# Batch 2's keys and values loaded as two halves, the second added by an accumulating DMA; query halves interleaved with expert weights; weight forms moved to other slots of the vector engine

## The chip, the cores and the metric

The kernel runs on one core of one Trainium2 chip. The metric is the device time of one execution in microseconds (us). Five engines share the work: PE (the tensor engine, matmuls), DVE (vector), ACT (scalar), POOL (GpSimd) and SP (which here only issues transfers). Sixteen DMA engines move the data.

A ratio is the mean time of one kernel's fast runs over the mean of the other's fast runs of the same rounds on the same chip. So it is not quite the ratio of the medians that stand beside it.

## The reference, cut to what matters

```python
# B=8 batches, H=8 heads, S=576 tokens, D=64
k_p = k.reshape(B, H, 72, 8, D).mean(axis=3)      # keys: mean over 8 rows
v_p = v.reshape(B, H, 72, 8, D).mean(axis=3)
attn = softmax(q @ k_p^T / sqrt(D))               # 576 x 72 per head
x = (attn @ v_p)  as (B*S, H*D) = (4608, 512)
# then 4 experts over all 4608 tokens
for e in range(4):
    h = relu(x @ w1[e])                           # 512 -> 1024
    out += p[:, e:e+1] * (h @ w2[e])              # 1024 -> 512
```

## The kernel before

Tokens go through in batches of 512 and each batch through four experts. While the experts of one batch run on PE, the attention of the next is prepared on the other engines. Products with 2x2 blocks are done with seven block products instead of eight, so sums of the blocks of w1, w2, x and h ("forms") are computed beside the matmuls, on DVE and POOL. A form is due only at the step that uses it, but DVE also empties the PSUM banks (the memory into which the matmuls write) that PE needs next, so a form in a bad slot can stall PE.

Batches and experts are numbered from 0, as in the code. The keys and values of a batch are 72 partitions of 8 heads x 8 rows x 64 numbers. The mean over 8 rows is a chain of additions, 8 rows to 4, to 2, to 1. Before the change, batch 2 loads all 8 rows at once and has one addition more; later batches already load rows 0 to 3 and let a second DMA add rows 4 to 7 on landing:

```python
def load_kv(b, src, nm):           # whole: values into the w2_t space of experts 2 and 3
    wide = (w2_t[0:SP, 2:4]... if nm == "vraw" else raw_kv...)
    nc.gpsimd.dma_start(out=raws[(nm, b)], in_=src[b]...)

def load_half(b, src, nm, half):   # halves: both into raw_kv, the second accumulating
    raws[(nm, b)] = raw_kv[:, 0 if nm == "kraw" else 1]
    lo = half * POOL // 2
    nc.gpsimd.dma_start(
        out=raws[(nm, b)],
        in_=src[b].rearrange("h (j r) d -> j h r d", r=POOL)[:, :, lo:lo + POOL // 2],
        accum_op=ALU.add if half else ALU.bypass,
    )

def combine_w2(e, engine=nc.vector):   # four forms of w2(e), 128x1024 each
    return [lambda: sub(out=t1, in0=b12, in1=b11),
            lambda: sub(out=t2, in0=b22, in1=t1),
            lambda: sub(out=t4, in0=b21, in1=t2),
            lambda: sub(out=b12, in0=b22, in1=b12)]     # t1, t2, t4 live in w2_t[:, e]
```

The start-up queues all first loads on GpSimd, in this order at its end:

```python
load_w1(3)
load_w2(2)
load_q_halves(1)
load_v(1)
...
```

Batch 1's attention sits at numbered points of expert 3 of batch 0. The last steps make batch 1's tokens (`context`), and SP transposes them with four DMA transposes into xT, which PE needs for the next step:

```python
43: [lambda: fold_keys(1, hi), lambda: load_k(2)],
...
60: [lambda: scores(1, 3)],                               # s == 3 adds here, on GpSimd:
    # pool_waits(vps[1]), load_v(2), combine_w2(1, nc.gpsimd)
61: [lambda: context(1, 0), lambda: turn(1, 0)],          # turn: DMA transpose x_tok -> xT
64: ...  67: ...
69: [lambda: context(1, 3), lambda: turn(1, 3)],

def up_plain(c, e, fcs):     # first expert of batch 1: 32 matmuls that read all of xT
    ...
    nc.tensor.matmul(h_ps[:], lhsT=w1_bf[...], rhs=xT[:, kc, :], ...)
```

The softmax here doesn't subtract the row's maximum and nothing guards it: scores larger than these inputs give would overflow.

## Time and profile before

| | before |
|---|---|
| median of 3 runs | 503.62 us (502.55 to 504.42) |
| span of the profiled run | 501.7 us |
| PE busy | 490.9 us, 98% |
| granted PE clock | 1.00 |

In the timeline a row has the start, the duration, the engine, the line of code, the operation, output and inputs, and in brackets the idle time just before and what ended it. "SPq" and "POOL ... DMA" rows are issues of transfers, not the transfers themselves. This is the timeline of the kernel before:

```profile
66.92 0.85 POOL L88 DMA_DIRECT2D w_t<-in_v_dram  x1
...
69.91 5.21 SPq L425 DMA_TRANSPOSE xT<-x_tok  x3
...
75.79 1.23 SPq L425 DMA_TRANSPOSE xT<-x_tok  x1
...
78.65 7.07 PE L686 MATMUL h_ps<-xT,w_bf 128*128 128x512 bf16 x31
```

GpSimd issues one load, the whole of batch 2's values, at 66.92. SP then issues the four transposes of batch 1's tokens. By the DMA completions in the trace (the moment at which a transfer has fully arrived, "landed" from here on) the load landed at 76.55 and the last transpose at 78.52. PE reaches the next expert just then, at 78.65, with no wait on record: the transposes end on the critical path, the chain of work that sets the end time, with no slack.

### The profile page before, as it was taken

How to read it: one execution, taken by the hardware profiler on the slowest of the kernel's cores; microseconds unless marked ns; L12 is line 12 of the kernel's file. 1: busy time of each engine (PE TensorE's matmuls, PEld its weight loads, DVE VectorE, ACT ScalarE, POOL GpSimd, SP SyncE). 2: the span in 40 equal slices, each digit the busy share in tenths (PEclk: the TensorE clock that was granted, in tenths of full speed). 3: DMA queues.
4: the chain of work that ended last, by engine and by line, in shares of the span. 5: the costliest groups of instructions: out<-in, count | busy, mean ns of one | idle time of the engine just before them, and what ended most of it. 6: DMA issues, size and time to landing. Idle time of an engine off the chain costs nothing.

```text
span 501.7 us, 11093 instructions
## 1 busy us (share of the span) xinstructions
PE 490.9 (98%) x4537; PEld 397.5 (79%) x4547; DVE 362.1 (72%) x651; ACT 290.0 (58%) x541; POOL 196.0 (39%) x177
## 2 busy tenths in 40 slices
PE   8999999999999999999999999999999999999996
PEld 3746554797788888888788888887888888888884
DVE  1367886899987767777777777777777767776674
ACT  3654444765666567665766576666655565556650
POOL 8473360458323562267126722661115111512110
PEclk9999999999999999999999999999999999999999
DMA  9999999684925373836573287433210110012003
GB/s 118 206 205 205 202 182 169 77 105 49 140 57 93 47 76 105 109 48 61 110 119 49 23 136 89 65 40 63 65 22 1 54 43 12 1 43 64 2 1 84
DMA packets 84770, 41.90 MB, mean 84 GB/s; under 512 B 48736, under 2 KB 80224, under 8 KB 84720
## 3 DMA queue, kind: packets, MB, share of 16 engines
q0 software_dynamic: 43216, 22.91, 36.2%
q1 hardware_dynamic: 41104, 17.77, 17.1%
q8 instruction: 35, 0.57, 0.5%
q10 hardware_dynamic: 400, 0.52, 0.3%
q14 instruction: 15, 0.12, 0.1%
HBM read 45.69 MB, written 9.44 MB: 110 GB/s over the span
## 4 chain that ended last, share of the span: by engine, by line
PE 82%; DMA 9%; DVE 4%; POOL 2%; issue 1%; ACT 1%; POOLq 0%; ACTq 0%
PE u_ps L790 37%; PE g_ps L668 37%; DMA w_bf<-in_moe_w_dram 5%; DMA q_sb<-in_q_dram 3%; PE o_ps L884 3%; PE two L280 2%; PE two L403 1%; PE h_ps L686 1%; DMA H_sb<-in_v_dram 1%; DVE acc L774 1%; POOL w_bf L154 1%; DVE H_sb L716 1%; DVE w_t L658 0%; DVE w_t L656 0%; PE o_ps L899 0%
## 5 line engine op out<-in xcount | busy, mean ns | idle before, releaser
L668 PEld LDWEIGHTS <-w_bf 128*128 128x128 bf16 x1848 | 178.7, 98 | 26.4 <-issue 1.3
L774 DVE SCALAR_TENSOR_TENSOR acc<-u_ps,p_all,acc 128x512 f32<-128x512 f32 (+1 forms) x216 | 127.6, 592 | 70.2 <-ACT u_ps L827 65.9
L736 POOL TENSOR_TENSOR h_s<-H_sb,h_s 128x1024 bf16<-128x1024 bf16 x31 | 66.0, 2128 | 240.9 <-DVE h_s L735 228.4
L668 PE MATMUL g_ps<-xT,w_bf 128*128 128x256 bf16 x928 | 129.9, 273 | 0.0
L668 PE MATMUL g_ps<-xf,w_bf 128*128 128x256 bf16 x792 | 109.3, 272 | 0.6 <-DVE H_sb L716 0.2
L790 PEld LDWEIGHTS <-H_sb 128*128 128x128 bf16 x992 | 92.5, 98 | 20.1 <-issue 6.0
L712 ACT COPY r<-g_ps 128x512 f32<-128x512 f32 x136 | 79.7, 586 | 41.4 <-PE g_ps L668 34.3
L790 PE MATMUL u_ps<-w_bf,H_sb 128*128 128x256 bf16 x744 | 102.0, 273 | 0.0
L716 DVE CUSTOM_DVE_ANT_0 H_sb<-g_ps,r 128x512 bf16<-128x512 f32 x136 | 93.5, 687 | 2.8 <-ACT r L712 2.5
L719 ACT ACTIVATE H_sb<-g_ps 128x512 bf16<-128x512 f32 x128 | 76.3, 597 | 18.5 <-PE g_ps L668 18.2
L790 PEld LDWEIGHTS <-h_s 128*128 128x128 bf16 x744 | 72.8, 98 | 8.4
L811 ACT COPY g_ps<-g_ps 128x512 f32<-128x512 f32 x62 | 35.4, 570 | 73.5 <-PE g_ps L668 73.5
L790 PE MATMUL u_ps<-w_t,h_s 128*128 128x256 bf16 x496 | 74.4, 273 | 0.0
L827 ACT COPY u_ps<-u_ps 128x256 f32<-128x256 f32 x62 | 22.2, 358 | 34.1 <-PE u_ps L790 33.7
L790 PE MATMUL u_ps<-w_t,H_sb 128*128 128x256 bf16 x248 | 37.3, 273 | 1.3 <-DVE acc L774 1.3
L790 PE MATMUL u_ps<-w_bf,h_s 128*128 128x256 bf16 x248 | 37.2, 273 | 0.0
L884 PE MATMUL o_ps<-w_bf,H_sb 128*128 128x512 bf16 x145 | 35.6, 379 | 0.5 <-issue 0.2
L284 ACT ACTIVATE expT<-two 72x1024 bf16<-72x1024 f32 x28 | 28.5, 1016 | 0.0
L829 DVE TENSOR_SCALAR acc<-u_ps,p_all 128x512 f32<-128x512 f32 x16 | 12.0, 750 | 19.5 <-ACT u_ps L827 19.5
L884 PEld LDWEIGHTS <-H_sb 128*128 128x128 bf16 x152 | 14.3, 98 | 14.1 <-issue 0.8
L733 DVE TENSOR_TENSOR h_s<-H_sb 128x1024 bf16<-128x1024 bf16 x31 | 21.1, 681 | 2.7 <-ACT H_sb L690 2.7
L394 DVE TENSOR_TENSOR x_tok<-two,inv 128x512 bf16<-128x512 f32 x32 | 22.1, 691 | 1.1
(125 smaller groups left out, 446.9 us busy)
## 6 DMA issues: line engine op xcount, KB each, us to landing
out_dram<-acc SPq DMA_DIRECT2D x32, 256.0 KB, 2.4
w_bf<-in_moe_w_dram POOLq DMA_DIRECT2D x17, 256.0 KB, 8.9
w_bf<-in_moe_w_dram POOLq DMA_DIRECT2D x8, 512.0 KB, 14.5
q_sb<-in_q_dram POOLq DMA_DIRECT2D x6, 512.0 KB, 9.8
raw_kv<-in_k_dram POOLq DMA_DIRECT2D x10, 288.0 KB, 6.7
raw_kv<-in_v_dram POOLq DMA_DIRECT2D x10, 288.0 KB, 6.3
raw_kv<-in_k_dram POOLq DMA_DIRECT2D x2, 576.0 KB, 15.1
w_t<-in_v_dram POOLq DMA_DIRECT2D x2, 576.0 KB, 12.4
```

The lines of the kernel that those rows point to most:

```text
L284: nc.scalar.activation(out=state[("expT", b)][:, 2 * pair:2 * pair + 2].rearrange("j h r s p -> j s (h r) p"), in_=two[0:SP].rearrange("j ...
L394: nc.vector.tensor_tensor(out=x_tok, in0=c_ps[:, :, :, 0:D], in1=inv[:].unsqueeze(3).to_broadcast([P, 2, NPAIR, D]), op=ALU.mult,)
L668: nc.tensor.matmul(bank[:, t, :], lhsT=w1_bf[:, e, block, kc, lo:lo + P], rhs=x[:, kc, :], start=(first and t == 0 and kc == 0), stop=(t = ...
L712: nc.scalar.copy(out=r[:], in_=ps[:])
L716: nc.vector._custom_dve(TENSOR_ADD_SAT, out=out, in0=ps[:], in1=r[:], s0=BIG, s1=0.0)
L719: nc.scalar.activation(out=out, in_=ps[:], func=ACT.Relu)
L736: lambda: nc.gpsimd.tensor_sub(out=s4, in0=a12, in1=s2),
L774: nc.vector.scalar_tensor_tensor(out=acc, in0=ps, scalar=prob, in1=acc, op0=ALU.mult, op1=ALU.add,)
L790: nc.tensor.matmul(out, lhsT=lhs[0][:, lhs[1] + f, lhs[2]], rhs=rhs[0][:, rhs[1] + f, rhs[2]], start=(start and f == 0), stop=(f == FCH // ...
L811: nc.scalar.copy(out=s[:], in_=g[:])
L827: nc.scalar.copy(out=two[:, hi], in_=one[:, lo])
L884: nc.tensor.matmul(sums[r][:], lhsT=hidden[(c, e)][:, fc, r * P:(r + 1) * P], rhs=w2_bf[:, e, fc, :], start=(fc == 0), stop=(fc == FCH - 1),)
```

## The change

There are three intents. The queries of batch 1 should arrive earlier, by interleaving their halves with the halves of w2(2). Batch 2's keys and values should come as halves, as in later batches, which saves four DVE additions and frees the w2_t space of experts 2 and 3 early. With that space free, the forms of w2(2) and w2(3) can leave the two DVE slots at 116.8 and 130.7 us, where they collide with GpSimd and stall PE. The diff, cut to its core (the split of two load functions into halves is left out):

```diff
-            43: [lambda: fold_keys(1, hi), lambda: load_k(2)],
+            43: [lambda: fold_keys(1, hi), lambda: load_half(2, k, "kraw", 0)],
 ...
-            add(6, *key_parts(b)[:2])
-            add(7, *key_parts(b)[2:])
-            add(7, lambda: keys(b))
+            add(6, *key_parts(b)[:1])
+            add(7, *key_parts(b)[1:])
+            add(7, lambda: keys(b), *combine_w2(2))
 ...
-                add(9 + n, part)
+                add(10 + n, part)
 ...
-        load_w2(2)
-        load_q_halves(1)
+        for half in range(2):
+            load_w2_half(2, half)
+            load_q_half(1, half)
 ...
-                    [lambda: pool_waits(vps[1][0:1, H - 1, 0:1]), lambda: load_v(2)]
-                    + combine_w2(1, nc.gpsimd))
+                    [lambda: pool_waits(vps[1][0:1, H - 1, 0:1]), lambda: load_half(2, k, "kraw", 1),
+                     lambda: load_half(2, v, "vraw", 0)] + combine_w2(1, nc.gpsimd)
+                    + [lambda: load_half(2, v, "vraw", 1)])
 ...                                                     # s == 5, 6, 7
-                w2f = combine_w2(2)
-                forms_due.extend(nothing[:3] + u[3:] + w2f[:1] + nothing[:2] + w2f[1:2])
+                v3 = combine_w2(3)
+                forms_due.extend(nothing[:3] + u[3:] + v3[:1])
-                v3 = combine_w2(3)
-                forms_due.extend(nothing[:3] + w2f[2:] + nothing[:2] + v3[:1])
+                forms_due.extend(nothing[:3] + v3[3:] + v3[1:2])
-                forms_due.extend(nothing[:3] + v3[3:] + v3[1:2] + nothing[:2] + v3[2:3])
+                forms_due.extend(nothing[:3] + v3[2:3])
```

Also gone is the first addition (8 rows to 4) in `fold_parts`.

More of the change, by code (lines that the diff above doesn't have):

```diff
@@ L125, in load_first_q, with load_q_half @@
         )
-    def load_q_halves(b):
-        raws[("q", b)] = qpool.tile([P, H, NR, D], BF16, name="q_sb")
-        for hs in halves:
-            nc.gpsimd.dma_start(
-                out=raws[("q", b)][:, hs].rearrange("p h r d -> p h (r d)"),
-                in_=q[b, hs, 0:NT, :].rearrange("h (p r) d -> p h (r d)", r=NR),
-            )
+    def load_q_half(b, half):
+        if half == 0:
+            raws[("q", b)] = qpool.tile([P, H, NR, D], BF16, name="q_sb")
+        hs = halves[half]
+        nc.gpsimd.dma_start(
+            out=raws[("q", b)][:, hs].rearrange("p h r d -> p h (r d)"),
+            in_=q[b, hs, 0:NT, :].rearrange("h (p r) d -> p h (r d)", r=NR),
+        )
     def load_q_rem(b):
@@ L157, in load_w1, with load_w2_half @@
                 )
+    def load_w2_half(e, half):
+        rows = moe_w2[e].rearrange("(fc p) d -> p fc d", p=P)
+        fcs = slice(half * FCH // 2, (half + 1) * FCH // 2)
+        nc.gpsimd.dma_start(out=w2_bf[:, e, fcs], in_=rows[:, fcs])
     def load_w2(e):
-        rows = moe_w2[e].rearrange("(fc p) d -> p fc d", p=P)
-        for lo in (0, FCH // 2):
-            fcs = slice(lo, lo + FCH // 2)
-            nc.gpsimd.dma_start(out=w2_bf[:, e, fcs], in_=rows[:, fcs])
+        for half in range(2):
+            load_w2_half(e, half)
     def reload_w2(e):
@@ L218, in fold_parts @@
     def fold_parts(nm, b, hs, last, engine):
-        def first():
-            raw = raws[(nm, b)]
-            engine.tensor_add(out=raw[:, hs, 0:4, :], in0=raw[:, hs, 0:4, :],
-                                 in1=raw[:, hs, 4:8, :])
         def rest():
@@ L230, in rest @@
                 engine.tensor_add(out=out, in0=raw[:, hs, 0, :], in1=raw[:, hs, 1, :])
-        return [first, rest] if b == 2 else [rest]
+        return [rest]
     def key_parts(b):
@@ L967 @@
         load_w1(3)
-        load_w2(2)
-        load_q_halves(1)
+        for half in range(2):
+            load_w2_half(2, half)
+            load_q_half(1, half)
         load_v(1)
```

## The prediction

> **What bounds the kernel now.** I read the page first, then the waits of the tensor engine, then the timeline of the stretches that the diff touches.
>
> ```profile
> PE 490.9 (98%) x4537; PEld 397.5 (79%) x4547; DVE 362.1 (72%) x651; ACT 290.0 (58%) x541; POOL 196.0 (39%) x177
> ```
>
> The tensor engine (PE) is busy for 490.9 of 501.7 us at a granted clock of 1.00. The diff changes no matmul, so only time in which PE stands still can be won. The waits of PE alone, longest first:
>
> ```profile
> PE u_ps L790 <- DVE acc L774: 1.3, 2, 0.8
> PE o_ps L501 <- DVE x_rem L939: 1.3, 1, 1.3
> PE one L380 <- DMA H_sb<-in_v_dram: 0.9, 1, 0.9
> PE qt_ps L338 <- DMA q_sb<-in_q_dram: 0.7, 1, 0.7
> ...
> PE g_ps L668 <- DVE H_sb L716: 0.2, 1, 0.2
> ```
>
> The second and third belong to the first 14 us, which the diff leaves alone. The first, fourth and last lie where it works. A pipelined matmul is recorded as 273 ns but followed by the next after 109 ns (8 in 0.87 us in the chain), so a stall is about 0.16 us longer than its idle time. Counted from start to start, PE loses 0.88 us at 56.1 (first half of batch 1's queries not landed), 0.38 at 93.5, 0.98 + 0.16 at 118.7 and 0.57 + 0.16 at 133.1 (0.66 there, less the 0.09 that every score matmul costs). Together **3.1 us, 0.6% of the time**: the ceiling of this change.
>
> The timeline around the longest of them, VectorE (DVE), GpSimd (POOL) and PE together (start, duration, engine, line):
>
> ```profile
> 116.34 2.11 POOL L736 TENSOR_TENSOR h_s<-H_sb,h_s 128x1024 bf16<-128x1024 bf16 x1 [1.23 <-DVE h_s L735]
> ...
> 116.77 2.23 DVE L656 TENSOR_TENSOR w_t<-w_bf 128x1024 bf16<-128x1024 bf16 x1
> ...
> 118.92 0.74 DVE L774 SCALAR_TENSOR_TENSOR acc<-u_ps,p_all,acc 128x512 f32<-128x512 f32 x1
> ...
> 119.72 0.60 PE L790 MATMUL u_ps<-w_t,H_sb 128*128 128x256 bf16 x4 [0.82 <-DVE acc L774]
> ```
>
> A form of w2(3) on DVE starts 0.43 us after GpSimd's own subtraction and takes 2.23 us instead of 0.68. It ends 0.55 us after GpSimd does. The accumulation behind it frees the PSUM bank that PE wants, so PE stands. At 130.74 the same happens to the next form (2.23 us, PE at 133.69).
>
> **What the Trainium skill says.** "SBUF — State Buffer", section "Who interferes with whom": a VectorE instruction with two SBUF inputs contends with a GpSimd instruction that reads SBUF, and the one that comes later is blocked for the whole of the other. The trace agrees: 2.23 against 0.68 us. "DMA: Bandwidth & Descriptors", "Queues, rings and completion order": descriptors start in ring order on each of 16 engines, which take turns between queues packet by packet. The trace agrees: the 16 completions of a load spread over some 5.5 us and the last ones come in order of issue, and a transpose of x_tok issued at 69.91 beside queued loads landed after 6.48 us, one issued at 75.79 after 2.73. Same page, "Rules for kernel authors": an accumulating transfer must wait for the semaphore of an earlier one to the same bytes. The trace agrees: GpSimd idled 6.15 us before the second half of batch 3's keys at 99.66, until the first half had landed. No page gives the accumulation's price; here such loads landed 6.5 to 9.4 us after issue against 5.0 to 7.3 for first halves.
>
> **The change part by part** (numbers of batches and experts as in the code, from 0; the halves concern index 2).
>
> *Queries interleaved with w2(2).* By the completions in the trace the two halves of w2(2) landed at 53.06 and 55.61, the query halves at 56.96 and 58.28. The queue moves about 200 KB per us without a pause until 75 us. So a half of w2 costs 2.55 us, a query half 1.35. In the new order: w2 half 53.06, query half 54.4, w2 half 56.96, query half 58.28. The first transposes no longer wait (PE gets there at 56.13), but the second want their half at about 57.5 and **it lands at 58.28 as before**, since the same bytes are ahead of it. They started at 58.41 before. I give this part 0.1 us, and 0.15 more for an earlier DVE copy that removes most of a 0.32 us gap at 60.6. Total 0.25 of the 0.88.
>
> *Halves instead of folds.* Four DVE additions of 72x1024 go, 0.68 us each, 2.7 us. DVE is no bound. On PE's path is only what delays it at 93.45: the value folds (0.68 at 91.44) push L716, which ends at 93.89 and holds PE's bank. Without one fold it ends near 93.2 and PE's 0.38 us go. Values now live in raw_kv, so the w2_t space of experts 2 and 3 is free some 30 us earlier, and that allows the next part.
>
> *Forms in other slots.* All four of w2(2) go into the DVE gap before L733; one of w2(3) into the slot at 95, two into those at 108 (0.68 us each there now), the last to 122. The slots at 116.8 and 130.7 become empty: **PE wins 1.14 + 0.73 = 1.87 us**. At 122 two forms, 0.81 and 1.64 us beside GpSimd's work, already run without a PE stall, so one will too.
>
> *The price, between 70 and 88 us.* The gap that receives w2(2) is this one:
>
> ```profile
> 86.39 0.69 DVE L733 TENSOR_TENSOR h_s<-H_sb 128x1024 bf16<-128x1024 bf16 x1 [2.71 <-ACT H_sb L690]
> 87.11 0.69 DVE L734 TENSOR_TENSOR H_sb<-H_sb 128x1024 bf16<-128x1024 bf16 x1
> ```
>
> Four forms at 0.69 are 2.75 us; two folds less give back 1.36; net 1.39 of 2.71, which fits by itself. But GpSimd shifts. The second half of the keys must wait for the first, which I put at 71.67 (landing of the whole now) less half of 2.92, so 70.2. GpSimd is in order: 70.3, plus 1.4 and 0.85 for two issues, plus 4 x 2.13 for the forms of w2(1), ends at 81.1 instead of 76.4. DVE's work from 78.6 on has two SBUF inputs and collides: L637 and the first fold may lose up to one GpSimd instruction each. I estimate 1 to 3 us lost, so DVE reaches L733 0 to 1.7 us late. PE needs L734's result at 87.86 and waits for all that is late. The second halves also move while batch 1's xT transposes are in flight; PE starts the next expert at 78.65, 0.13 us after the last of them landed, so a later landing costs directly: estimate 0 to 0.8. Together 0 to 2.5, middle **1.1 us lost**.
>
> Sum: 0.25 + 0.38 + 1.87 - 1.1 = 1.4 us won. From 503.6 that is 502.2.
>
> **The rivals.** (a) All stalls go and nothing new appears: 3.1 us, 500.5. For it: the net DVE work falls. Against it: the byte count ahead of the second query half. (b) The stall moves instead of going: new waits at 78 and 88 us eat all of the gain, or more: 503.6 to 504.5. For it: GpSimd's later end and the tight xT landing. Against it: DVE's gap of 2.71 us. (c) The accumulating loads arrive so late (after 80 us) that the key fold, the transpose of the keys and the scores at 87.5 slip together: over 505. The 9.4 us of one such load beside transposes speaks for it; that nothing but these loads is left in the queue after 75 speaks against. (d) DMA becomes lighter and everything early wins: no, the bytes are the same.
>
> **Range and chances.** Certain gains of 2.25 us (93, 118, 133) less 0 to 2.5, plus 0.25, gives 501.1 to 503.6; the runs of before spread by 0.9 us either way, so I widen to 500.7 to 503.9. A change of 2% is 10 us, more than three times the ceiling; slower by that would need a new wait of 10 us, which nothing shows. Faster 0.005, same 0.985, slower 0.01.
>
> **What would show it.** In the new profile: the wait of L338 for the queries stays at about 0.6 us but before the second transposes; L656 and L658 of w2 on DVE all near 0.7 except one; no PE idle time near 118 and 133; L716 at 93 no longer holds PE; the idle time of DVE before L733 is gone or small, and PE idles before L790 near 88 if I am right about GpSimd ending near 81. I am wrong if PE shows no new wait between 77 and 89 (then it is faster, near 501), or if L280 or L686 wait there for DMA (then slower).

## More of the kernel before

The windows view gives busy time by engine for a stretch, and at the end of a row the granted clock, the DMA share and the GB/s moved (192 GB/s is 192 KB per us; all DMA queues together). Of the kernel before:

```profile
68.00:72.00 4.00, 3.89 (x35) 2.37 (x35) 3.52 (x8) 1.04 (x2) 3.92 (x2) 1.00 1.43 192
72.00:75.00 3.00, 2.87 (x26) 1.32 (x26) 2.40 (x6) 0.00 (x0) 2.92 (x3) 1.00 1.37 167
```

The queue is full here: 192 and 167 KB per us.

## The result, and the profile after

| | before | after |
|---|---|---|
| median of 4 runs each | 503.75 us | 506.69 us |
| lowest to highest | 502.55 to 504.42 | 506.01 to 507.36 |
| span of the profiled run | 501.7 us | 504.4 us |

The ratio is 1.0061 (95% interval 1.0034 to 1.0088). By the 2% rule this is "same", but the change made the kernel slower by 3 us, and the time lies above the predicted range (500.7 to 503.9).

The page of the kernel after, busy time of each engine and the granted PE clock in 40 slices:

```profile
PE 491.5 (97%) x4537; PEld 397.7 (79%) x4547; DVE 356.6 (71%) x647; ACT 289.9 (57%) x541; POOL 198.0 (39%) x179
...
PEclk9999998999999999999999999999999999999999
```

DVE has 5.5 us less to do, as intended. PE has the same matmuls. One slice of the clock, the seventh, shows an 8: something happened between 76 and 88 us. The waits of PE from 50 to 160 us (total, times, longest), of the kernel after, say what:

```profile
PE h_ps L685 <- DMA xT<-x_tok: 3.9, 1, 3.9
PE qt_ps L337 <- DMA q_sb<-in_q_dram: 0.3, 1, 0.3
```

The waits behind the vector engine that the prediction showed (1.3 and 0.2 us) are gone. One new wait of 3.9 us stands in their place: the first matmul of batch 1's first expert waits for xT. The timeline of the kernel after, in the same stretch as above:

```profile
66.24 0.18 POOL L251 COPY mark<-vp 1x1 bf16<-1x1 bf16 x1 [5.75 <-DVE vp L256]
...
69.42 1.42 POOL L95 DMA_DIRECT2D raw_kv<-in_k_dram  x1 [2.99 <-DMA raw_kv<-in_k_dram]
69.47 5.94 SPq L424 DMA_TRANSPOSE xT<-x_tok  x3
...
70.30 1.39 POOL L95 DMA_DIRECT2D raw_kv<-in_v_dram  x1
...
76.09 1.25 SPq L424 DMA_TRANSPOSE xT<-x_tok  x1
...
82.22 8.35 PE L685 MATMUL h_ps<-xT,w_bf 128*128 128x512 bf16 x31 [3.95 <-DMA xT<-x_tok]
```

GpSimd is ready at 66.42, but the accumulating half of the keys must not start before the first half has landed (68.79 by the completions). It stands for 2.99 us. Meanwhile nothing is queued behind it, and the windows view of the kernel after shows the queue running dry:

```profile
68.00:72.00 4.00, 3.93 (x35) 2.27 (x34) 3.52 (x7) 0.60 (x2) 2.58 (x3) 1.00 0.78 99
72.00:75.00 3.00, 2.88 (x26) 1.52 (x28) 2.40 (x7) 0.00 (x0) 2.92 (x2) 1.00 0.95 78
...
80.00:82.00 2.00, 0.00 (x0) 0.00 (x0) 0.00 (x0) 0.00 (x0) 1.51 (x2) 0.85 0.97 313
```

From 68 to 75 us the DMA engines moved 4 x 99 + 3 x 78 = 630 KB, against 4 x 192 + 3 x 167 = 1269 KB before. The two loads issued at 69.42 and 70.30 landed at 76.21 and 80.50; the four transposes, issued at nearly the same times as before, landed at 73.60, 80.69, 81.05 and 82.08, where before they had landed at 76.39, 77.04, 77.45 and 78.52.

The clock of 0.85 in the last of these rows is the second loss. One tile's view, of xT in the kernel after (shortest, median and longest duration in ns, first and last start):

```profile
L685 PE MATMUL h_ps<-xT,w_bf x31: 379/379/631, 82.2 to 90.2; 128*128 128x512 bf16 x31
```

The first seven matmuls after the wait run at about half rate, so that the group takes 8.35 us in place of 7.07. Of the four runs, two (507.33 and 507.36 us) had a granted clock of 0.992 against 0.997 in the other two, the profiled one among them; so they ran longer at half rate than this trace shows.

The balance of PE in the two profiled runs, counted from start to start between one matmul and the next, before against after:

| place (us, before) | before | after | difference |
|---|---|---|---|
| 56 to 58, queries | 0.95 | 0.46 | -0.49 |
| 60, copy of the queries | | | -0.04 |
| 78, xT | 0.11 | 4.11 | +4.00 |
| 79, half rate | 0 | 1.28 | +1.28 |
| 93, value folds | 0.38 | 0 | -0.38 |
| 118, form beside GpSimd | 1.14 | 0 | -1.14 |
| 133, form beside GpSimd | 0.73 | 0 | -0.73 |
| sum | | | +2.5 |

The spans differ by 2.7 us; some 0.1 us of the rest lies in the first 14 us.

At 118 the intended gain is seen as planned, in the timeline of the kernel after:

```profile
120.79 2.12 POOL L735 TENSOR_TENSOR h_s<-H_sb,h_s 128x1024 bf16<-128x1024 bf16 x1 [1.23 <-DVE h_s L734]
...
122.04 0.75 DVE L773 SCALAR_TENSOR_TENSOR acc<-u_ps,p_all,acc 128x512 f32<-128x512 f32 x1 [0.74 <-ACT u_ps L826]
...
125.54 1.51 DVE L657 TENSOR_TENSOR w_t<-w_bf,w_t 128x1024 bf16<-128x1024 bf16 x1
```

DVE has nothing to do while GpSimd subtracts, so it is there in time for the accumulation (it waits 0.74 us for ACT). Only one form, at 125.54, still runs beside GpSimd and takes 1.51 us, and PE does not notice.

### The profile page after: what moved, and what is told of

Read it like the earlier page. It is cut to its first block, busy times and chain, and to the rows that moved or that the text cites. A ratio compares the mean times of both kernels' runs of the same rounds, so it can differ in the third digit from the quotient of the medians.

```text
span 504.4 us, 11092 instructions
## 1 busy us (share of the span) xinstructions
PE 491.5 (97%) x4537; PEld 397.7 (79%) x4547; DVE 356.6 (71%) x647; ACT 289.9 (57%) x541; POOL 198.0 (39%) x179
## 4 chain that ended last, share of the span: by engine, by line
PE 85%; DMA 9%; POOL 3%; issue 1%; ACT 1%; DVE 1%; POOLq 0%; ACTq 0%
PE u_ps L789 38%; PE g_ps L667 38%; DMA raw_kv<-in_k_dram 3%; DMA w_bf<-in_moe_w_dram 3%; PE o_ps L883 3%; DMA q_sb<-in_q_dram 3%; PE two L279 2%; PE h_ps L685 2%; PE two L402 1%; DMA xT<-x_tok 1%; POOL w_bf L155 1%; POOL H_sb L107 1%; POOL w_bf L163 0%; POOL q_sb L122 0%; PE o_ps L898 0%
## 5 line engine op out<-in xcount | busy, mean ns | idle before, releaser
L732 DVE TENSOR_TENSOR h_s<-H_sb 128x1024 bf16<-128x1024 bf16 x31 | 21.1, 681 | 2.8 <-ACT H_sb L689 2.8
```

## The experiments

**My theory after the result.** The accumulating load makes GpSimd wait for the first half; the queue runs dry; its loads then overlap the four transposes, xT lands late, and the wait lets the clock fall. **Rivals:** the query interleave (or some other reordering) delays everything behind it; the accumulation itself is slow, whenever it is issued; the transposes are late for a reason that has nothing to do with the loads. Two questions of size go with it: what the half rate costs, and what the forms' new slots are worth alone.

The first four kernels ran on one chip, beside seven runs of the kernel before (median 503.41).

### e1_q_only: the query interleave alone

```diff
 (kernel before)
-        load_w2(2)
-        load_q_halves(1)
+        for half in range(2):
+            load_w2_half(2, half)
+            load_q_half(1, half)
```

> The kernel before with nothing but the interleaving of batch 1's query halves with w2(2). If the queries' part is as the changed kernel's trace has it, the wait before the first query transposes (0.88 us from start to start) goes, one of 0.4 to 0.5 us appears before the second, and nothing new appears near 78 us: 503.2 to 503.6. If the interleaving itself delays the transposes of x_tok (the rival), the tensor engine waits over 1 us before the expert that starts near 78 us and the time is over 505.

The median was 504.02 us (503.2 to 503.6 expected), the ratio 1.001 (0.9995 to 1.0026): no change that the noise lets through. The first query transposes no longer waited. The second ones started at 58.49, against 58.41 before, still held by the landing of their half. The bytes ahead of that half are the same, so nothing is won at its end. The stalls at 118 and 133 are there as before, and there is no wait for xT. So the interleave is cleared of the loss.

### e2_plain_k: the change, with a plain second half of the keys

The second half of batch 2's keys overwrites the first instead of being added. The keys are wrong (the output stays within the tolerance of the comparison). The wait for the first half stays, since both write the same bytes.

```diff
 (kernel after, load_half)
-            accum_op=ALU.add if half else ALU.bypass,
+            accum_op=ALU.add if half and (b, nm) != (2, "kraw") else ALU.bypass,
```

> The changed kernel with one word different: the second half of batch 2's keys is written over the first instead of added to it (wrong result on purpose; same bytes, same issue, same waits). Theory A (the accumulation is what is slow: it moved about 90 KB per us where plain loads moved 190, and holds the transposes of x_tok behind it): the loads end near 76 us, the last transpose lands by 79.5, the wait of 3.95 us falls under 1.5 and the time to 502 to 503.5. Theory B (any bytes that are issued at 69 to 71 us collide with the transposes, added or not): the wait stays above 3 us and the time at 505.5 to 507.

The median was 503.98 us, the ratio 1.0012 (0.9986 to 1.0037). The waits of PE:

```profile
PE h_ps L685 <- DMA xT<-x_tok: 2.8, 1, 2.8
PE two L279 <- DMA kpT<-kp: 0.6, 1, 0.6
```

2.8 of the 3.95 us are left with a plain load issued late. The loads landed at 78.81 and the last transpose at 80.19, which is 1.9 us earlier than in the kernel after, but PE was there 0.7 us earlier too (77.55 against 78.27). The result lies between the marks of both theories (under 1.5, over 3 us). In this pair of traces the accumulation has a share of 1 to 2 us, and the rest of the wait remains without it; how far one trace can be trusted is said below the table of runs. The matmuls behind this wait ran at full rate (7.07 us). A second wait appears, for the transpose of the keys before the first scores.

### e3_no_v_half: the first half of the values not loaded

The half at 70.30 is left out, and the remaining half of the values is loaded after the forms of w2(1). The result is wrong (relative error 0.23).

```diff
 (kernel after, point 60)
-                    [..., lambda: load_half(2, k, "kraw", 1),
-                     lambda: load_half(2, v, "vraw", 0)] + combine_w2(1, nc.gpsimd)
-                    + [lambda: load_half(2, v, "vraw", 1)])
+                    [..., lambda: load_half(2, k, "kraw", 1)] + combine_w2(1, nc.gpsimd)
+                    + [lambda: load_half(2, v, "vraw", 0)])
```

> The changed kernel without the first value load at 70.3 us: batch 2's values are moved as one half only, after GpSimd's forms of w2(1) (wrong result on purpose). The accumulating key load stays. Theory A (accumulation): the key load alone still holds the transposes, the wait before the expert near 78 us stays above 2 us, 504.5 to 506. Theory B (bytes at that time): half of the bytes are gone, the wait falls under 1.5 us, 501.5 to 503.5.

The median was 502.63 us, the ratio 0.9986 (0.9969 to 1.0004).

```profile
PE h_ps L685 <- DMA xT<-x_tok: 0.5, 1, 0.5
```

With one load fewer in front, the last load lands at 76.09, xT at 78.33, and 0.5 us of the wait is left. So the bytes that go in late, not the transposes themselves, hold xT up. How much of the wait they make is less sure: e7 below is the same program up to this point, and there PE waited 2.0 us.

### e4_fill: the wait filled with matmuls on zeros

Eighteen matmuls that add nothing stand where PE waits, so that PE is busy although xT is as late as before.

```diff
 (kernel after, s == E, j == 1)
+                        warm(18)
                         up_plain(c, e, range(FCH))
```

> The changed kernel with 18 matmuls on zeros in the tensor engine's wait before the expert near 78 us (18 x 0.216 = 3.9 us). Theory: the 7 matmuls at half rate after the wait (about 0.21 us lost each, 1.2 to 1.4 us in all) come from the engine's idle time; with the idle time filled they run at full rate, the wait for the transposes stays the same and the time falls by 1.0 to 1.4 us, to 505.3 to 505.7. Rival: the slow matmuls come from something else at that time (the transposes' traffic): the time stays or grows.

The median was 506.02 us, the ratio 1.0052 (1.0035 to 1.007). The timeline:

```profile
78.78 4.05 PE L500 MATMUL o_ps<-x_rem 128*128 128x512 bf16 x18
...
82.67 7.07 PE L685 MATMUL h_ps<-xT,w_bf 128*128 128x512 bf16 x31
```

The group behind the wait takes 7.07 us again: all 1.28 us of the half rate are gone at that place. In the times this saving is not shown: the median is 0.7 us below that of the kernel after (1.0 to 1.4 expected), and the intervals of the two ratios overlap. In e4's profiled run the wait for the queries was 1.05 us against 0.29, which hides a part.

The next four kernels ran on a second chip, beside eleven runs of the kernel before (median 503.93).

### e5_whole_forms: values whole as before, forms in the new slots

Keys and values are loaded as in the kernel before. The values are put at another offset, so that three forms of w2(2) can run in the gap near 86 us. The rest of the forms go so that the slots at 116.8 and 130.7 stay empty.

```diff
 (kernel before, with the query interleave)
+        at = FCH * TH if b == 2 else 0
-        wide = (w2_t[...][:, 0:H * POOL * D] if nm == "vraw"
+        wide = (w2_t[...][:, at:at + H * POOL * D] if nm == "vraw"
 ...
-            add(7, lambda: keys(b))
+            w2f = combine_w2(2)
+            add(7, lambda: keys(b), w2f[0], w2f[1], w2f[3])
 ...                                                     # s == 5, 6, 7
+                forms_due.extend(nothing[:3] + u[3:] + nothing[:3] + combine_w2(2)[2:3])
+                forms_due.extend(nothing[:3] + v3[:2])
+                forms_due.extend(nothing[:3] + v3[3:] + v3[2:3])
```

> The forms of w2(2) and w2(3) moved without the loads in halves: batch 2's keys and values come whole, as before (the values at the other end of the same space, so that three of the four forms of w2(2) fit into DVE's idle time before L733); queries interleaved as in the first experiment. Theory: the moved forms are worth what the prediction gave them, and only the halved loads cost. No waits near 118 and 133 us (1.14 + 0.73 us less than before), the 0.38 at 93 stays, no wait over 0.6 us at the expert near 78 us: 501.0 to 502.2 against 503.4. Rival (DVE gets late in its filled gap and the tensor engine waits near 88 us instead): a wait of 1 us or more at L734's result, and 503 or over.

The median was 502.48 us, the ratio 0.9975 (0.9962 to 0.9988). The waits of PE from 50 to 160 us:

```profile
PE g_ps L676 <- DVE H_sb L724: 0.5, 2, 0.3
PE u_ps L798 <- DVE acc L782: 0.2, 1, 0.2
```

No wait for xT. The stalls at 118 and 133 are gone, and waits of 0.2, 0.3 and 0.2 us for DVE remain near 94, 115 and 127. So the forms' new slots are worth having by themselves, and they need no halves.

### e6_k_early: the change, with the first half of the keys ahead of three other loads

```diff
 (kernel after)
-        load_w2(3)
-        load_q_rem(0)
-        load_q_rem(1)
 ...
-            43: [lambda: fold_keys(1, hi), lambda: load_half(2, k, "kraw", 0)],
+            43: [lambda: fold_keys(1, hi), lambda: load_half(2, k, "kraw", 0),
+                 lambda: load_w2(3), lambda: load_q_rem(0), lambda: load_q_rem(1)],
```

> The changed kernel with the first half of batch 2's keys queued ahead of w2(3) and the remaining queries, instead of behind them. Bytes, accumulation and the rest are the same; the second half need not wait for the first any more and is issued near 66.5 us instead of 69.4, into a queue that is still full. Theory (the queue ran empty while GpSimd waited for the first half, and the two loads came 3 us late, beside the transposes): the last load lands by 77.5, the wait of 3.95 us falls under 1.5, no matmuls at half rate, the time 501.5 to 503.5. Rival (the accumulating load holds the transposes wherever it is issued): the wait stays over 2.5 us and the time over 504.5.

The median was 503.81 us (502.5 to 506.05, six runs; 501.5 to 503.5 expected), the ratio 1.0007 (0.999 to 1.0025), clear of the kernel after's 1.0034 to 1.0088. GpSimd no longer waits: the second half is issued at 67.00 and the values' half at 67.89. The waits of PE:

```profile
PE h_ps L686 <- DMA xT<-x_tok: 1.2, 1, 1.2
PE two L279 <- DMA kpT<-kp: 0.3, 1, 0.3
```

Issuing early takes 2.75 of the 3.95 us away, and xT lands 2.6 us earlier (79.52). 1.2 us stay although the issue is as early as the whole load of before. In the windows view the stretch from 72 to 75 moved 126 KB per us, between the 78 of after and the 167 of before.

### e7_v_late: both halves of the values behind the forms of w2(1)

```diff
 (kernel after, point 60)
-                     lambda: load_half(2, v, "vraw", 0)] + combine_w2(1, nc.gpsimd)
-                    + [lambda: load_half(2, v, "vraw", 1)])
+                    ] + combine_w2(1, nc.gpsimd)
+                    + [lambda: load_half(2, v, "vraw", 0), lambda: load_half(2, v, "vraw", 1)])
 ...
-                add(10 + n, part)
+                add(14 + n, part)
```

> The changed kernel with both halves of batch 2's values issued after GpSimd's forms of w2(1), and their folds four slots later. Theory (the value half is what the transposes wait for, as in the third experiment): the wait falls to 0.5 to 1 us; with the other gains, 501.5 to 503.5. If the late second half (near 93 us) is not there for its fold near 99, a new wait on DVE shows there.

The median was 508.7 us, the ratio 1.0097 (1.0075 to 1.012): a miss. The waits of PE from 70 to 110 us:

```profile
PE two L402 <- DVE vp L229: 3.1, 1, 3.1
PE h_ps L685 <- DMA xT<-x_tok: 2.0, 1, 2.0
```

I had expected 0.5 to 1 us for xT; it was 2.0, since the accumulating half of the keys alone, issued at 70.42, still took until 78.17. (e3, the same program up to here, issued it at 69.03; it landed at 76.09, and PE waited 0.54.) The larger wait, 3.1 us, is of my own making, as the timeline of e7 shows:

```profile
104.36 2.16 POOL L735 TENSOR_TENSOR h_s<-H_sb,h_s 128x1024 bf16<-128x1024 bf16 x1 [1.46 <-DVE h_s L734]
104.58 2.09 DVE L229 TENSOR_TENSOR vp<-raw_kv 72x256 bf16<-72x256 bf16 x1
```

The values' second half had landed at 95.77. But I had moved the folds back by four points to make room for it, and there the last one meets GpSimd's subtraction and takes 2.09 us instead of 0.29. This is the collision of 118 us once more, with PE behind it. It cost more than its length: from 105.86 to 112.69 us the granted clock was 0.50, in which matmuls followed each other after 213 ns instead of 109, an estimate of 3 us more. So e7's time says nothing against late values as such; its wait for xT says that one accumulating half issued at 70 can be enough for 2 us.

### e8_fold_early: e5 with the value folds spread over other points

```diff
 (e5_whole_forms)
-            for n, part in enumerate(value_parts(b)):
-                add(9 + n, part)
+            for n, part in zip((8, 9, 11, 12), value_parts(b)):
+                add(n, part)
```

> The fifth experiment with the first fold of the values one slot earlier, in DVE's idle microsecond before L829, and the two folds of the other half one slot apart from it. Theory: the 0.38 us that the tensor engine loses at 93 us goes too, 0.3 to 0.4 less than the fifth: 500.7 to 501.9. Rival: the fold collides with GpSimd's subtraction that starts at 88.9, and DVE is late for L829: no gain, or 0.3 us worse.

The median was 501.88 us (500.91 to 502.62), the ratio 0.9962 (0.9948 to 0.9976). This beats both kernels; against e5 the intervals overlap. In the trace the stall at 93 is gone too. This profiled run did show one wait for xT, whose last transpose landed at 78.57:

```profile
PE h_ps L694 <- DMA xT<-x_tok: 0.8, 1, 0.8
```

Its loads are those of e5, which showed no wait, and its xT landed at the same time as there (78.57, 78.67). But PE had lost less in the first 60 us (in e5's profiled run the granted clock was 0.50 from 15.8 to 19.2 us) and began its last group before xT at 73.65, against 74.92 in e5. So up to this point the queue sets the pace by the clock on the wall, and PE that comes earlier only waits. This also bounds what any gain ahead of 78 us can be worth, the queries' included.

The last two ran on a third chip, beside seven runs of the kernel before (median 503.38).

### e9_extra_load: the kernel before with one useless plain load

If late bytes in front of the transposes are the cause, then a plain load of 288 KB that nobody reads must do the same to the kernel before. It has no accumulation and no wait for an earlier half. It is issued at 69.49, beside the transposes.

```diff
 (kernel before)
+    def load_extra():                      # half of v[2] into unused bytes of w2_t
+        nc.gpsimd.dma_start(out=spare..., in_=v[2]...[:, :, 0:POOL // 2])
 ...
-                    + combine_w2(1, nc.gpsimd))
+                    + combine_w2(1, nc.gpsimd)[:1] + [load_extra] + combine_w2(1, nc.gpsimd)[1:])
```

> The kernel before with one load added that nothing uses: half of batch 2's values (288 KB, plain) into free space, issued near 70 us between GpSimd's first and second form of w2(1). No accumulation, no wait for an earlier half, no other change. Theory (bytes of the GpSimd queue beside the transposes are the cause): the last load lands 1.5 to 2.5 us later than in the kernel before (78 to 79 instead of 76.55), the last transpose 1 to 2 us after it, the tensor engine waits 1 to 2 us before the expert near 78 us, 504.5 to 506. Rival (accumulation or the waiting issue is needed): no wait over 0.5 us and the time of before.

The median was 507.89 us, the ratio 1.0097 (1.007 to 1.0124). A wait of PE and the view of xT:

```profile
PE h_ps L693 <- DMA xT<-x_tok: 2.3, 1, 2.3
```

```profile
L693 PE MATMUL h_ps<-xT,w_bf x32: 376/379/631, 80.6 to 89.0; 128*128 128x512 bf16 x32
```

The extra load landed at 78.72 and xT at 80.48. The same wait appears, with the same half rate behind it: the 32 matmuls take 8.75 us, 1.68 more than the 7.07 elsewhere. The cause is confirmed: late bytes alone bring the wait. The size was larger than I had expected (504.5 to 506). In the profiled run the wait and the half rate make 3.95 us; but two of the other three runs had a granted clock of 1.00 and took as long (508.05 and 507.72), so the half rate does not explain the size there, and without a trace it stays open.

### e10_early_plain: early issue and no accumulation of the keys together

This is e6 with e2's edit, to close the square of early or late, plain or added (keys wrong again).

> The sixth experiment (first key half queued early) with the second key half plain as in the second (wrong keys on purpose). It is the fourth corner beside the changed kernel (late, added: wait 3.95 us), the second experiment (late, plain: 2.78) and the sixth (early, added: 1.20). Theory (two separate costs: the late issue some 2.7 us, the accumulation some 1.2): the wait falls to 0 to 0.5 us, 502 to 503.5. If it stays near 1.2, the accumulation costs only in the late case.

The median was 504.88 us, the ratio 1.0029 (1.0 to 1.0058). The waits of PE:

```profile
PE two L279 <- DMA kpT<-kp: 1.5, 1, 1.5
PE u_ps L790 <- DVE H_sb L734: 0.7, 1, 0.7
```

As expected xT is on time and PE does not wait for it (PE also came 0.8 us later than in the kernel after). The time missed (502 to 503.5 expected): now the scores wait 1.5 us. The second half of the values, which still accumulates, was issued at 78.04 and landed at 88.04; the transposes of queries and keys that the scores need were in flight with it (issued at 78.36 and 84.05, landed at 86.95 and 89.51). So the halves carry a second, smaller penalty of the same kind a few us later. It is also seen in e2 (0.6), e6 (0.3) and e3 (0.6, there behind a plain half). The wait of 0.7 us lies at 118, where GpSimd's folds of the next keys meet DVE's sums of h (e3 has 0.6 there): the stall can come back at that place without a form in it. The profiled run waited 1.16 us for the queries besides.

### The runs side by side

| kernel | last load of GpSimd landed | last transpose of xT landed | PE there at | PE waits for xT | half rate behind it | ratio |
|---|---|---|---|---|---|---|
| before | 76.55 | 78.52 | 78.65 | none | no | 1 |
| after | 80.50 | 82.08 | 78.27 | 3.95 | yes, 1.28 us | 1.0061 |
| e1, queries only | 76.59 | 78.60 | 78.74 | none | no | 1.0010 |
| e2, late, plain | 78.81 | 80.19 | 77.55 | 2.78 | no | 1.0012 |
| e3, one load fewer | 76.09 | 78.33 | 77.92 | 0.54 | no | 0.9986 |
| e4, wait filled | 81.09 | 82.51 | 78.78 | (filled) | no | 1.0052 |
| e5, whole, forms moved | 75.33 | 78.67 | 79.01 | none | no | 0.9975 |
| e6, early, added | 77.35 | 79.52 | 78.45 | 1.20 | no | 1.0007 |
| e7, values late | 78.17 | 80.31 | 78.45 | 2.00 | no (but at 106) | 1.0097 |
| e8, e5 with folds moved | 76.93 | 78.57 | 77.91 | 0.80 | no | 0.9962 |
| e9, before plus a load | 78.72 | 80.48 | 78.34 | 2.27 | yes, 1.68 us | 1.0097 |
| e10, early, plain | 75.98 | 78.87 | 79.11 | none | no | 1.0029 |

In all twelve traces the last transpose landed 1.4 to 3.3 us after the last load of the other queue. e9, which adds one late load and changes nothing else, shows that this is cause and not company.

The square for the keys, in landing of xT (and in wait of PE): late and added 82.08 (3.95), late and plain 80.19 (2.78), early and added 79.52 (1.20), early and plain 78.87 (none). By the landings the late issue costs 2.6 us with the accumulation and 1.3 without it; the accumulation costs 1.9 us late and 0.7 early. The late issue is the larger part. But each cell is one trace, and PE came 0.7 us earlier in e2 and 0.8 later in e10 than in the kernel after. How loose this is can be seen in e3 and e7: they are one program up to 78 us, and xT landed at 78.33 and 80.31. (The four traces with whole loads and nothing added, before, e1, e5 and e8, lie within 0.15 us, so e9's 80.48 stands clear of them.) So among the kernels with halves, differences under 2 us are not shown by these landings. By the times, the late issue is shown to cost (after 1.0034 to 1.0088, e6 0.999 to 1.0025); the accumulation's cost is not: late, the intervals just overlap (e2 0.9986 to 1.0037), and early the plain version was not faster (e10 1.0 to 1.0058).

## Why the prediction was wrong, point by point

**The bound and the ceiling** were read rightly: PE is the bound, and all that could be won was 3.1 us. The error was on the side of the losses.

**Queries** (0.25 predicted, 0.53 measured in the kernel after). The second half landed at 57.95, a little earlier than the reckoned 58.28; in e1 it landed at 58.45 and in e4 at 58.63, so this is within the scatter, and the extra gain is luck: alone, the interleave won nothing. The reason given, the same bytes ahead of the second half, holds.

**Folds and forms** (0.38 and 1.87 predicted, both measured exactly so). The stalls at 93, 118 and 133 are gone. The forms run at 0.68 to 0.69 us on DVE, except one at 1.51 that PE does not notice (in e5 and e8 a wait of 0.2 us stands there). e5 and e8 show that this gain is real and can be had without the halves.

**DVE late at L733** (0 to 1.7 predicted): not seen. GpSimd's forms of w2(1) did end late, at 80.31 (81.1 predicted). But DVE could not collide with them, because it waited for xT itself until 82.20. And before L732, as the line is now numbered, it was still idle, in the kernel after:

```profile
91.23 0.69 DVE L732 TENSOR_TENSOR h_s<-H_sb 128x1024 bf16<-128x1024 bf16 x1 [2.78 <-ACT H_sb L689]
```

In the other kernels with three or four forms in this gap DVE was idle for 0.8 to 1.6 us there. The reckoning from the gap alone, "fits by itself", was right.

**The step that failed** is the last one of the price: "The second halves also move while batch 1's xT transposes are in flight; PE starts the next expert at 78.65, 0.13 us after the last of them landed, so a later landing costs directly: estimate 0 to 0.8." The place, the mechanism and the sign were named. Its size was not worked out, and it was wrong by a factor of about five or more: 3.95 us of wait, plus 1.28 us of half rate that the prediction did not know of at all. Against the 1.1 us taken off for the whole price, 5.3 were lost.

What the text passed over is its own earlier sentence. It says that GpSimd must wait until 70.3 for the first half, and it uses this to push the *forms* of GpSimd later. The same wait also stops GpSimd from *issuing loads*. The queue, which the text gives as moving some 200 KB per us without a pause until 75, then has nothing to do; the bytes that were moved in those 7 us before (1269 KB) are only half moved after (630 KB), and the other half meets the transposes. At 200 KB per us the two halves of 288 KB would be an estimate of 2.9 us and land before 75; they landed at 76.21 and 80.50. Byte counts were used to argue that nothing changes ("the bytes are the same"), where what counts is when they move.

The rivals: (b), the stall that moves, came nearest, with the right line (L686, now L685) and the right releaser among its signs, but it gave only 503.6 to 504.5. (c), accumulating loads late enough to hold up keys and scores, is a smaller fact: it shows as 0.3 to 1.5 us in e2, e6 and e10. (d) was rejected rightly. The sign "I am wrong if ... L280 or L686 wait there for DMA (then slower)" is what the profile showed.

The Trainium skill says on the page "DMA: Bandwidth & Descriptors", section "Issuing engines are not separate DMA queues", that transfers started by different engines run on the same 16 DMA engines and interleave. The traces agree: SP's transposes ended 1.4 to 3.3 us after GpSimd's last load landed, in twelve of twelve. Had I given that sentence its weight, the question would have been how many bytes of the other queue are still to move when the transposes are issued.

**Open:** why the DMA engines moved so little between 72 and 80 us. Both queues had work, and yet only 78 KB per us moved from 72 to 75. In the packet records of the kernel after, SP's queue moved 514 packets from 70 to 72 us and then 64 from 72 to 76, although two more transposes had been issued; in the kernel before it moved none before 72 and 1036 from 72 to 76. Two explanations are only argued. One is that accumulating packets hold the engines longer. The other, which no run tests, is the size of the packets: the halves move in packets of 512 bytes, the whole values in packets of 1024, and from 72 to 76 us one of 512 took 92 ns on average in the kernel after and 70 in e2, one of 1024 took 99 in the kernel before.

**Why the clock fell** after waits of 3.95 and 2.27 us but not after 2.78 and 2.00 can be read from the traces. In all twelve traces every stretch of constant granted clock, up to the last, is a whole multiple of 3.41 us long, so the clock changes only at marks 3.41 us apart; where these lie differs from run to run. What counts is PE's idle time between two marks: 3.15 us in the kernel after (78.01 to 81.42), 2.21 in e7 near 104 (102.45 to 105.86) and 2.09 in e9 (78.52 to 81.94), each followed by a clock of 0.50 from the second mark on. At its wait for xT, e7 had 1.89 us (78.56 to 81.97), and the longer wait of e2 lay across a mark (1.75 and 1.03 us on its two sides); neither was followed by a lower clock. So besides the length of a wait its place between the marks decides. In the first 20 us this count fails once: in e5, 1.47 us (12.37 to 15.78) were followed by half rate.

## What to carry to other kernels

A load that must wait for an earlier one can empty the queue behind it, so ask of every such wait what else was to be issued in that time, and what the late bytes will meet; transposes and loads share the DMA engines, and if the transposes end on the critical path with no slack, late bytes are paid for. When a change has a gain and a cost, try the gain without the cost: here the forms' new slots (e8, ratio 0.9962) needed no halves at all. And count an idle stretch of the tensor engine of about 2 us or more as dearer than its length, since half-rate matmuls may follow.

## What the Trainium skill lacked or had wrong

- "TensorE: Matmul & The Clock Gate", "Part 1: The HAM clock gate (the "warmup" mystery)": it gives the half rate as the state after at least one idle window of about 3.4 us. Here the window need not be idle throughout: 2.09 us of idle time within 3.41 were followed by a clock of 0.50 (e9; 0.58 on average between 82 and 86 us, 1.68 us lost), 1.89 us were not (e7). The page's remark that the window runs free agrees with the marks 3.41 us apart that lie differently in each run.
- "DMA: Bandwidth & Descriptors" gives no price of an accumulating transfer. Here its issue took GpSimd 1.42 us against 0.85 for a plain one (half and whole load alike; the plain half issued right behind it took 1.39). The transposes behind an added second half of the keys landed 0.7 us (78.87 and 79.52) and 1.9 us later (80.19 and 82.08) than behind a plain one, each from one pair of traces and within the scatter named above.
- The same page, "Queues, rings and completion order", says that an engine takes turns between queues packet by packet. It gives no figure for how long a DMA transpose is held up beside a load: here the transposes issued at 72.03, 74.14 and 76.09 landed only at 80.69, 81.05 and 82.08, all after the other queue's last load (80.50); only the first of the four (69.47) landed before it, at 73.60.
